# A decode step of sliding-window attention mixed with a gated MLP: TensorE's loop over all eight key sets, wide last products, and two rows of wo loaded by DMAs of 121 and 7 partitions

## The chip, the cores and the metric

One core of a Trainium2 chip. The metric is the device time of one execution in microseconds, the median of several runs of the program. The engines are TensorE (PE, whose weight loads the profile lists as PEld), VectorE (DVE), ScalarE (ACT), GpSimd (POOL) and SyncE (SP). Here SP does nothing but issue the large loads, in order, and 16 DMA engines carry them out.

## The reference

```python
# B = 4, one query token, D = 512; 32 query heads, 8 key heads of 128, the last 4096 of 16384 keys; F = 1792
q = (x @ wq) -> [B, 32, 1, 128];  k, v = repeat of the last 4096 rows of each cache, 4 query heads to a key head
p = softmax(q @ k.T * 128 ** -0.5);   a = (p @ v) -> [B, 1, 4096] @ wo
gate = x @ W_gate;  gate = gate * (gate > 0);   b = (gate * (x @ W_up)) @ W_down
g = sigmoid((x * gate_w).sum(-1, keepdims=True))
return g * a + (1 - g) * b
```

All inputs and the output [4, 1, 512] are bf16.

## The kernel before

The work on the caches is cut into eight **sets** (`NSET`): set `s` is one batch element and half of its eight key heads, 4 MB of keys and 4 MB of values. Each cache has two buffers of 4 MB in SBUF (`Ksb`, `Vsb`), used in turn.

**The load queue.** SP issues in this order: wq (into `Wbig`, ahead of everything else), K0, K1, V0, K2, V1, ..., K7, V6, W_gate and W_up (into the place of an even K), V7, W_down (into the place of an even V), then wo into `Wbig` in pieces of 16, 10 and 4 rows a partition (`WO_CUTS`, L245) and two half-width pieces of the last 2 rows (L248). A load of K for set s waits for the last scores of set s-2 (`SC`, L222), a load of V for the last value products of set s-2 (`PV`, L226). The first loads into a buffer wait for nothing. SP is in order, so a load that waits holds back all behind it.

**A set on the engines.** `kt` (L363): 64 fp32 transposes of 128x128 turn the keys (two bf16 seen as one fp32) on PE, four to a PSUM bank; ACT (L368) or DVE (L370) copies each bank back over the keys. `scores` (L384): four banks of 8 products 32x512; DVE adds a mask and takes the maximum (L392). `maximum` (L398 to L403) finds one maximum for each row, with one product on PE. `exponent` (ACT, L411) and `turn` (a DVE transpose, L418) prepare the weights of the set before in two halves, `values` (L429) multiplies them with V in four groups of 16 products, ACT copies the result (L435), and `combine` (L443, L447, L450, L451) sums and scales it into `oq`. One set's transposes and scores are interleaved with the exponents and values of the set before, and the combine of the one before that; the order is written out by hand.

**PE's program.** `Program` collects each engine's operations with the semaphore values that they wait for. The operations of sets 0 and 1 stand in PE's program one by one; sets 2 to 7 are a hardware loop of three turns, two sets to a turn (`LOOP_FIRST`, `LOOP_TURNS`, `turn_edge`, `emit`, L134). At the end of a turn PE drains and takes a turn's counts off the semaphores. The other engines' programs have no loop.

**Ahead of the sets.** POOL builds identities, masks and zeroed tiles. x and the gate's row are widened, transposed by PE, and copied by DVE into `gwB` and `xT`; PE then computes the gate (ACT's sigmoid) and q: 32 products with wq (L314), a copy by ACT (L324), transposes (L332), copies by DVE and ACT (L338).

**The end.** After set 7's loop part: its exponents, `gateup` (L459) with W_gate and W_up, ReLU and product on ACT and DVE, the value products of set 7, its combine. Then `product` (L530) adds 14 rows of W_down and 32 rows of wo to one PSUM bank `AB`: for each row four products, one to each quarter of the 512 columns, on four column groups of PE:

```python
        for i in range(NFT):
            for cb in range(4):
                product(hT[:, 4 * i:4 * i + 4], Wd[:, i, :], cb, i == 0, False, None,
                        [("WD",), ("H",), ("SCC", NSET - 1, NBANK - 1)])
        for k in range(len(WO_CUTS) - 1):
            for i in range(WO_CUTS[k], WO_CUTS[k + 1]):
                for cb in range(4):
                    product(oq3[:, :, i], Wo3[:, i, :], cb, False, False, None, [("WO", k), ("OQ", NSET - 1)])
```

DVE and ACT copy the four quarters to `outr`, and SP stores it (L574).

Of the kernel before, what the change touches and what calls it, by code (L numbers as in the profile page):

```python
# [31 lines left out]
WO_CUTS = (0, 16, 26, 30)  # L32
ACT_TAKES = (0, 1, 4, 6, 8, 9, 11, 12, 13, 14, 15)
LOOP_FIRST = 2
LOOP_TURNS = 3


class Program:

# [8 lines left out]
    def __init__(self):  # L48
        self.ops = {e: [] for e in self.ENGINES}
        self.events = {}  # L50
        self.counts = {}
        self.history = {}
        self.dmas = []
        self.turns = []
        self.shared = {}

    def op(self, engine, fn, name=None, waits=(), sem=None):
        if name is not None:
            assert name not in self.events, name
            sem = sem or engine  # L60
            self.counts[sem] = self.counts.get(sem, 0) + 1
            self.events[name] = (sem, self.counts[sem], engine, len(self.ops[engine]))
            self.history.setdefault(sem, []).append(len(self.ops[engine]))
        self.ops[engine].append((fn, name, tuple(waits), False))

# [12 lines left out]
    def need(self, engine, waits):  # L78
        need = {}
        for w in waits:  # L80
            if w is None:
                continue
            s, n, by, at = self.events[w]
            for own, mine in (("dve", "vd"), ("act", "va")):
                want = mine if engine == "pe" else own
                if by == own and s in (own, mine) and s != want:
                    s = want
                    n = 1 + sum(1 for k in self.history[s] if k < at)
                    assert n <= self.counts[s], w
            need[s] = max(need.get(s, 0), n)  # L90
# [6 lines left out]
    def emit_list(self, eng, sems, engine, ops, shift, seen):  # L97
        for fn, name, waits, is_dma in ops:
# [5 lines left out]
            if fn is None:  # L104
                continue
# [17 lines left out]
    def emit(self, engine, eng, sems):  # L123
# [6 lines left out]
        first = self.signature(ops[t[0]:t[1]], {})  # L130
        for k in range(1, len(t) - 1):
            shift = {s: k * n for s, n in self.lowered.items() if s not in self.shared}
            assert self.signature(ops[t[k]:t[k + 1]], shift) == first, k
        with eng.Fori(0, len(t) - 1):  # L134
            self.emit_list(eng, sems, engine, ops[t[0]:t[1]], {}, {})
# [3 lines left out]
        shift = {s: (len(t) - 1) * n for s, n in self.lowered.items() if s not in self.shared}  # L139
        self.emit_list(eng, sems, engine, ops[t[-1]:], shift, {})  # L140


def bass_gated_mix__sliding_block_cached__glu_gated_reglu__decode_kernel(
# [13 lines left out]
    with ExitStack() as ctx:  # L157
# [7 lines left out]
        pT = sb("pT", [128, 2, 2048], BF16)  # L165
# [11 lines left out]
        xT = sb("xT", [128, 4, 32], BF16)  # L177
        xw = sb("xw", [5, 512], FP32)
        gwB = sb("gwB", [128, 512], BF16)
        gsb = sb("gsb", [128, 8], FP32)  # L180
        qW = sb("qW", [128, NSET, 2, 32], BF16)
        qS = sb("qS", [128, 2, 2, 32], BF16)
        mx = sb("mx", [128, 2, NBANK], FP32)
        mcol = sb("mcol", [128, 2], FP32)
# [3 lines left out]
        rowsum = sb("rowsum", [128, 2, NPIECE], FP32)  # L188
        osb = sb("osb", [128, 2, 256], FP32)
# [5 lines left out]
        hT = sb("hT", [128, NFT * 4], BF16)  # L195
        outr = sb("outr", [4, 512], BF16)
        banks = [ctx.enter_context(nc.psum_tensor("bank%d" % i, [128, 512], FP32)) for i in range(8)]
# [9 lines left out]
        Wq3 = Wbig[:, :].rearrange("p (t w) -> p t w", t=4)  # L207
# [4 lines left out]
        def loop_sem(kind, s):  # L212
            if kind == "K" and s >= LOOP_FIRST or kind == "V" and LOOP_FIRST - 1 <= s < NSET - 1:
# [11 lines left out]
        def load_v(s):  # L225
            P.dma("sp", lambda e: e.dma_start(Vsb[:, s % 2, :], heads(A_v_cache, s)), ("V", s),  # L226
                  [("PV", s - 2, 3)] if s >= 2 else [], sem=loop_sem("V", s))
# [14 lines left out]
        wo_src = A_wo.rearrange("(p i) w -> p (i w)", p=128)  # L242
        for k in range(len(WO_CUTS) - 1):
            lo, hi = 512 * WO_CUTS[k], 512 * WO_CUTS[k + 1]
            P.dma("sp", lambda e, lo=lo, hi=hi: e.dma_start(Wbig[:, lo:hi], wo_src[:, lo:hi]), ("WO", k), [("Q",)])  # L245
        wo_src3 = A_wo.rearrange("(p i) w -> p i w", p=128)
        for u in range(2):
            P.dma("sp", lambda e, u=u: e.dma_start(Wo3[:, WO_CUTS[-1]:32, 256 * u:256 * u + 256],  # L248
                                                   wo_src3[:, WO_CUTS[-1]:32, 256 * u:256 * u + 256]), ("WOL", u), [("Q",)])
# [8 lines left out]
        P.op("pool", lambda e: e.memset(xw[:, :], 0.0), ("XW0",))  # L258
        P.op("pool", lambda e: e.memset(xT[:, :, :].rearrange("p t r -> p (t r)"), 0.0))
        P.op("pool", lambda e: e.memset(qW[:, :, :, :].rearrange("p s h w -> p (s h w)"), 0.0), ("QZ",))  # L260
# [34 lines left out]
        for t in range(4):  # L295
            P.op("pe", lambda e, t=t: e.transpose(FB[:, t * 8:t * 8 + 5], xv[0:5, t, :], identw[0:5, 0:5]),  # L296
                 ("XT",) if t == 3 else None, [("XW",), ("IDENTW",)])
        P.op("dve", lambda e: e.tensor_copy(gwB[:, :].rearrange("p (t m) -> p t m", t=4),
                                            fx[:, :, 4:5].to_broadcast([128, 4, 128])),
             None, [("XT",)])  # L300
        P.op("dve", lambda e: e.tensor_copy(xT[:, :, 0:4], fx[:, :, 0:4]), ("XTC",), [("XT",), ("QZ",)], sem="vd")
        for t in range(4):
            P.op("pe", lambda e, t=t: e.matmul(FB[:, 32:36], gwB[:, t * 128:(t + 1) * 128], xT[:, t, 0:4],
                                               start=(t == 0), stop=(t == 3)),
                 ("Z",) if t == 3 else None, [("XTC",)])
# [31 lines left out]
        for cc in range(2):  # L337
            P.op(("dve", "act")[cc], lambda e, cc=cc: (e.copy if cc else e.tensor_copy)(  # L338
                qW[64 * cc:64 * cc + 64, :, :, 16 * cc:16 * cc + 16].rearrange("p s o j -> p (s o) j"),
                FB[64 * cc:64 * cc + 64, 64:320].rearrange("p (k j) -> p k j", j=16)),  # L340
                ("QC", cc), [("QT",), ("QZ",)])
# [5 lines left out]
        fills = []  # L347

        def copy_done(f):
            return ("KTC",) + fills[f]  # L350

        def kt(s, i):
            f = len(fills)
            fills.append((s, i))
            bk = TR[f % NTR]
            for cc in range(4):
                c = 4 * i + cc
                w = []
                if cc == 0:
                    w = [("K", s), ("IDENTW",)] + ([copy_done(f - NTR)] if f >= NTR else [])  # L360
                    if i == NTR - 1 and s >= 1:
                        w.append(("NEGMAX", s - 1))
# [9 lines left out]
        def scores(s, bank):  # L372
# [4 lines left out]
            for o in range(2):  # L377
                for a in range(4):
                    w = []
                    if a == 0 and o == 0:  # L380
                        w = [("KTC", s, 4 * bank + u) for u in range(4)] + [("QS", s)]
                        if prev >= 0:
                            w.append(("SCC", prev // NBANK, prev % NBANK))
# [12 lines left out]
        def maximum(s):  # L396
            par = s % 2
            P.op("dve", lambda e: e.tensor_reduce(mcol[:, par:par + 1], mx[:, par, :], AXIS.X, ALU.max),  # L398
                 ("MCOL", s), [("SCC", s, NBANK - 1), ("MT", s - 2) if s >= 2 else None], sem="vd")
            P.op("pe", lambda e: e.matmul(TR[NTR - 1][:, 0:128], mcol[:, par:par + 1].to_broadcast([128, 128]), identw[:, :],  # L400
                                          start=True, stop=True),
                 ("MT", s), [("MCOL", s), ("KTC", s, NFILL - 1)])
            P.op("dve", lambda e: e.tensor_tensor_reduce(  # L403
                mrow[:, :], TR[NTR - 1][:, 0:128], qmask[:, :], -SCALE, -LOWEST, ALU.add, ALU.min, negmax[:, par:par + 1]),
# [4 lines left out]
        def exponent(s, k):  # L409
            par = s % 2  # L410
            P.op("act", lambda e: e.activation(  # L411
                sc[:, par, k * PW:(k + 1) * PW], sc[:, par, k * PW:(k + 1) * PW], ACTF.Exp,
                bias=negmax[:, par:par + 1], scale=SCALE, accum_out=rowsum[:, par, k:k + 1]),
                ("EXP", s, k), [("NEGMAX", s), ("SUMS", s - 2) if s >= 2 else None])

        def turn(s, k):
            par = s % 2
            P.op("dve", lambda e: e.transpose(pT[:, par, k * PW:(k + 1) * PW], sc[:, par, k * PW:(k + 1) * PW]),  # L418
                 ("PTT", s, k), [("EXP", s, k), ("PV", s - 2, 3) if s >= 2 else None], sem="vd")

        def values(s, k):
            par = s % 2
            for c in range(16):
                g = c % 4
                w = []
                if c == 0:
                    w = [("PTT", s, k * NPIECE // 4), ("V", s), ("OSB", s - 1) if s >= 1 else None]
# [6 lines left out]
            if k == 3:  # L434
                P.op("act", lambda e: e.copy(osb[:, par, :], OB[:, 0:256]), ("OSB", s),  # L435
                     [("PV", s, 3), ("SUMS", s - 2) if s >= 2 else None], sem="va")

        def combine(s):
            par, b, half = s % 2, s // 2, s % 2
            r = slice(64 * half, 64 * half + 64)  # L440
            for k in range(8):
# [3 lines left out]
                     [("OSB", s), ("WSUM",), ("OQ", s - 1) if s >= 1 else None])  # L445
            for k in range(NPIECE):
                P.op("pe", lambda e, k=k: e.matmul(FB[r, 416:417], Wsum[:, :], rowsum[:, par, k:k + 1],  # L447
                                                   start=(k == 0), stop=(k == NPIECE - 1)),
                     ("SUMS", s) if k == NPIECE - 1 else None, [])
            P.op("dve", lambda e: e.reciprocal(recip[r, par:par + 1], FB[r, 416:417]), ("RECIP", s), [("SUMS", s)])  # L450
# [4 lines left out]
        def gateup():  # L455
            for which, W, key in ((0, Wg, "WG"), (1, Wu, "WU")):
                for t in range(4):
                    for g in range(4):
# [4 lines left out]
                            [(key,)] + [copy_done(f) for f in range(NSET * NFILL - NTR, NSET * NFILL)])  # L463
# [7 lines left out]
                hT[:, :].rearrange("p (i b) -> p i b", b=4),  # L471
# [5 lines left out]
        for i in range(NFILL):  # L477
            kt(0, i)
            if i % 4 == 3 and i > 3:
                scores(0, i // 4 - 1)  # L480
        scores(0, 3)
        for s in range(1, NSET):
            if s >= LOOP_FIRST and (s - LOOP_FIRST) % 2 == 0:
# [12 lines left out]
            if s >= 2:  # L496
                combine(s - 2)
# [35 lines left out]
        for i in range(NFT):  # L533
            for cb in range(4):
                product(hT[:, 4 * i:4 * i + 4], Wd[:, i, :], cb, i == 0, False, None,
                        [("WD",), ("H",), ("SCC", NSET - 1, NBANK - 1)])
        for k in range(len(WO_CUTS) - 1):
            for i in range(WO_CUTS[k], WO_CUTS[k + 1]):
                for cb in range(4):
                    product(oq3[:, :, i], Wo3[:, i, :], cb, False, False, None, [("WO", k), ("OQ", NSET - 1)])  # L540
# [12 lines left out]
        per = {}  # L553
        for s in ("vd", "va"):
            eng = {"vd": "dve", "va": "act"}[s]
            a = P.events[("KTC", LOOP_FIRST, next(i for i in range(NFILL) if (i in ACT_TAKES) == (s == "va")))][1]
            b = P.events[("KTC", LOOP_FIRST + 2, next(i for i in range(NFILL) if (i in ACT_TAKES) == (s == "va")))][1]
            per[s] = b - a
        per["pq"] = 2
# [3 lines left out]
        P.lowered = per  # L563

# [3 lines left out]
        nc.sync.dma_start(Wbig[:, :], A_wq.rearrange("(p t) w -> p (t w)", p=128)).then_inc(sems["wq"], 16)  # L568
# [51 lines left out]
```

## Time and profile before

| | |
|---|---|
| median of 3 runs | 196.13 us (196.07 to 196.14) |
| the profiled execution | 196.17 us, of which the trace spans 194.9 |
| TensorE products, weight loads | 139.4 us (72%), 103.6 us (53%) |
| VectorE, ScalarE, GpSimd | 77.2 us (40%), 76.1 us (39%), 9.5 us (5%) |
| loaded from HBM | 81.01 MB, 416 GB/s over the span |
| mean granted clock of TensorE | 0.889 |

The shares are of the span. In the profile's rows of 40 slices each digit is the busy share of a slice in tenths; a slice is 4.9 us. A line of the timeline gives the start and the duration in us, the engine, the line of the kernel, the operation, output and inputs, the number of instructions, and in brackets how long the engine was idle before it and what released it. `SPq` is SP's queue issuing a DMA. In the queue list, q1 carries the loads that SP issues, q8 and q14 are queues that fetch instructions.

### The profile page before, as it was taken

What the parts mean: (1) busy time and instruction counts of PE and PEld (TensorE: products, weight loads), DVE (VectorE), ACT (ScalarE), POOL (GpSimd) and SP (SyncE); (2) the same over time, 40 slices, a digit from 0 to 9 for tenths busy, and PEclk for the clock granted to TensorE, in tenths of its full rate; (3) what the DMA queues carried; (4) which work ended last, traced back from release to release, by engine and by line L of the source; (5) the groups of instructions that cost most, each with busy time, mean ns of one, the idle gap of its engine ahead of it and who ended that gap; (6) DMA issues with size and microseconds to landing.
All of it is one profiled execution on the core that took longest, in us unless ns stands there. A gap on an engine that the chain in (4) does not pass through costs nothing.

```text
span 194.9 us, 3931 instructions
## 1 busy us (share of the span) xinstructions
PE 139.4 (72%) x1728; PEld 103.6 (53%) x1728; DVE 77.2 (40%) x169; ACT 76.1 (39%) x140; POOL 9.5 (5%) x41
## 2 busy tenths in 40 slices
PE   0135399688789818996898189995995899643834
PEld 0112397366468517763685177854773777422633
DVE  0100045477268302762583026623952456280101
ACT  2005136494285404462854043445641545240001
POOL 8700000000000000000000000000000000000000
PEclk9999999999999995899999855799999579995855
DMA  6999999999999999999999999999999999998993
GB/s 216 444 437 430 430 444 434 430 430 430 440 430 417 437 427 430 437 437 427 430 430 444 430 437 430 430 430 430 430 430 430 430 386 427 479 430 381 429 397 102
DMA packets 3884, 81.16 MB, mean 416 GB/s; under 512 B 409, under 2 KB 930, under 8 KB 1058
## 3 DMA queue, kind: packets, MB, share of 16 engines
q1 hardware_dynamic: 3864, 81.01, 97.3%
q8 instruction: 8, 0.13, 0.3%
q14 instruction: 2, 0.02, 0.0%
q10 hardware_dynamic: 10, 0.01, 0.0%
HBM read 81.01 MB, written 0.00 MB: 416 GB/s over the span
## 4 chain that ended last, share of the span: by engine, by line
DMA 55%; PE 36%; ACT 4%; DVE 3%; issue 1%; SPq 1%; DVEq 0%
DMA Ksb<-in_A_k_cache_dram 43%; PE bank L363 23%; DMA Wbig<-in_A_wo_dram 11%; PE bank L384 6%; ACT Ksb L368 3%; PE bank L429 2%; PE bank L443 2%; DVE Ksb L370 1%; PE bank L530 1%; ACT L411 1%; ACT sc L411 1%; DVE pT L418 1%; PE bank L447 0%; DVE sc L392 0%; PE bank L400 0%
## 5 line engine op out<-in xcount | busy, mean ns | idle before, releaser
L363 PE MATMUL bank<-identw,Ksb 128*128 128x128 f32 x512 | 77.0, 307 | 20.8 <-DMA Ksb<-in_A_k_cache_dram 14.9
L363 PEld LDWEIGHTS bank<-identw,Ksb 128*128 128x128 f32 x512 | 65.3, 158 | 31.6 <-DMA Ksb<-in_A_k_cache_dram 15.8
L368 ACT COPY Ksb<-bank 128x512 f32<-128x512 f32 x88 | 48.7, 589 | 73.0 <-PE bank L363 73.0
L370 DVE COPY Ksb<-bank 128x512 f32<-128x512 f32 x40 | 27.3, 684 | 40.6 <-PE bank L363 40.6
L392 DVE CUSTOM_DVE_ANT_0 sc<-bank,mask 128x512 bf16<-128x512 f32 x32 | 21.8, 682 | 28.8 <-PE bank L384 28.8
L429 PE MATMUL bank<-Vsb,pT 128*32 128x256 bf16 x512 | 20.9, 291 | 6.1 <-DMA Vsb<-in_A_v_cache_dram 6.1
L384 PE MATMUL bank<-Ksb,qS 128*32 128x512 bf16 x256 | 21.0, 405 | 1.8 <-ACT Ksb L368 0.9
L418 DVE STREAM_TRANSPOSE pT<-sc 128x1024 bf16<-128x1024 bf16 x16 | 19.7, 1236 | 2.1 <-ACT sc L411 2.0
L429 PEld LDWEIGHTS bank<-Vsb,pT 128*32 128x32 bf16 x512 | 13.3, 101 | 12.6 <-issue 8.8
L411 ACT ACTIVATE sc<-sc,negmax 128x1024 bf16<-128x1024 bf16 x16 | 18.4, 1151 | 1.9 <-DVE negmax L403 1.8
L443 PEld LDWEIGHTS bank<-osb,Wsel 128*64 128x64 f32 x128 | 9.4, 157 | 4.8 <-issue 3.7
L443 PE MATMUL bank<-osb,Wsel 128*64 128x32 f32 x128 | 10.3, 239 | 0.5 <-ACT osb L435 0.5
L435 ACT COPY osb<-bank 128x256 f32<-128x256 f32 x8 | 3.0, 373 | 17.6 <-PE bank L429 17.6
L400 PE MATMUL bank<-identw,mcol 128*128 128x128 f32 x16 | 3.8, 320 | 7.8 <-DVE mcol L398 4.7
L384 PEld LDWEIGHTS bank<-Ksb,qS 128*32 128x32 bf16 x256 | 4.1, 95 | 9.0 <-ACT Ksb L368 5.7
L400 PEld LDWEIGHTS bank<-identw,mcol 128*128 128x128 f32 x16 | 2.4, 187 | 10.2 <-DVE mcol L398 8.4
L343 POOL COPY qS<-qW 128x64 bf16<-128x64 bf16 x8 | 1.8, 238 | 120.5 <-PE bank L384 110.8
L530 PE MATMUL bank<-Wbig,oq 128*4 128x128 bf16 x128 | 4.2, 307 | 3.8 <-DMA Wbig<-in_A_wo_dram 3.8
L296 PE MATMUL bank<-identw,xw 5*128 5x5 f32 x4 | 0.6, 263 | 8.6 <-DVE xw L290 8.6
L450 DVE RECIPROCAL recip<-bank 64x1 f32<-64x1 f32 x8 | 1.3, 159 | 11.4 <-PE bank L447 11.4
L530 PEld LDWEIGHTS bank<-Wbig,oq 128*4 128x4 bf16 x128 | 3.1, 118 | 4.8 <-DMA Wbig<-in_A_wo_dram 4.7
L314 PE MATMUL bank<-Wbig,xT 128*32 128x512 bf16 x32 | 3.6, 631 | 2.7 <-DMA Wbig<-in_A_wq_dram 2.7
(55 smaller groups left out, 45.4 us busy)
## 6 DMA issues: line engine op xcount, KB each, us to landing
Ksb<-in_A_k_cache_dram SPq DMA_DIRECT2D x8, 4096.0 KB, 21.8
Vsb<-in_A_v_cache_dram SPq DMA_DIRECT2D x8, 4096.0 KB, 30.9
Wbig<-in_A_wq_dram SPq DMA_DIRECT2D x1, 4096.0 KB, 12.2
Wbig<-in_A_wo_dram SPq DMA_DIRECT2D x1, 2048.0 KB, 19.5
Ksb<-in_B_W_gate_dram SPq DMA_DIRECT2D x1, 1792.0 KB, 17.1
Ksb<-in_B_W_up_dram SPq DMA_DIRECT2D x1, 1792.0 KB, 21.0
Vsb<-in_B_W_down_dram SPq DMA_DIRECT2D x1, 1792.0 KB, 15.0
Wbig<-in_A_wo_dram SPq DMA_DIRECT2D x1, 1280.0 KB, 22.1
```

The costliest lines, as they stand in the source:

```text
L314: P.op("pe", lambda e, half=half, t=t, g=g, col=col: e.matmul(SCB[half][32 * g:32 * g + 32, 0:512], xT[:, t, :], Wq3[:, t, col:col + 512], ...
L363: P.op("pe", lambda e, bk=bk, cc=cc, c=c, s=s: e.transpose(bk[:, cc * 128:(cc + 1) * 128], Kw[:, s % 2, c * 128:(c + 1) * 128], identw[:, :]),
L368: P.op("act", lambda e: e.copy(dst, bk[:, :]), ("KTC", s, i), [("KT", s, i)], sem="va")
L370: P.op("dve", lambda e: e.tensor_copy(dst, bk[:, :]), ("KTC", s, i), [("KT", s, i)], sem="vd")
L384: P.op("pe", lambda e, a=a, o=o: e.matmul(bk[32 * a:32 * a + 32, 0:512], qS[:, s % 2, o, :], k4[:, 16 * bank:16 * bank + 16, 32 * a:32 * a ...
L392: P.op("dve", lambda e: e.tensor_tensor_reduce(sc[:, s % 2, bank * 512:(bank + 1) * 512], bk[:, :], mask[:, :], 1.0, LOWEST, ALU.add, ALU.max,
L400: P.op("pe", lambda e: e.matmul(TR[NTR - 1][:, 0:128], mcol[:, par:par + 1].to_broadcast([128, 128]), identw[:, :], start=True, stop=True) ...
L411: P.op("act", lambda e: e.activation(sc[:, par, k * PW:(k + 1) * PW], sc[:, par, k * PW:(k + 1) * PW], ACTF.Exp, bias=negmax[:, par:par + ...
L418: P.op("dve", lambda e: e.transpose(pT[:, par, k * PW:(k + 1) * PW], sc[:, par, k * PW:(k + 1) * PW]), ("PTT", s, k), [("EXP", s, k), ("PV ...
L429: P.op("pe", lambda e, c=c, g=g, blk=blk: e.matmul(OB[32 * g:32 * g + 32, 0:256], pT[:, par, 32 * blk:32 * blk + 32], Vsb[:, par, 256 * bl ...
L443: P.op("pe", lambda e, k=k, lo=lo: e.matmul(FB[r, 384:416], Wsel[:, lo:lo + 64], osb[:, par, 32 * k:32 * k + 32], start=(k == 0), stop=(k ...
L530: P.op("pe", lambda e: e.matmul(AB[32 * cb:32 * cb + 4, 0:128], stat, mov[:, 128 * cb:128 * cb + 128], start=start, stop=stop, tile_positi ...
```

## The change

- PE's loop now covers all sets: four turns of two sets. For the first turn, sets -2 and -1 are given as blanks: PE runs their products on a tile `zs` that POOL has zeroed in one memset, and DVE and ACT execute a 1-element instruction where an operation of a blank set would only raise a semaphore (`signal`, `blank`). PE adds a turn's counts to some semaphores before the loop (`ahead`).
- wq is loaded into the second V buffer instead of `Wbig`, so V1's load waits for the value products of blank set -1, and wo's loads wait for nothing.
- The product of `maximum` goes to a score bank, and the first scores of a set wait for it instead of the fourth bank of transposes.
- W_down and the first 16 rows of wo are multiplied in products of 512 columns, row n on column group n % 4 of a bank of its own; ACT copies that bank to `bulk`, and four fp32 products with `S32` add its four groups to `AB`, queued after the rows 26 to 29 of wo.
- The first two of wo's 16 rows a partition come by DMAs of their own, one for partitions 0 to 120 and one for 121 to 127, ahead of a DMA with the other 14.
- The copies to `gwB`, `xT` and both of q's move to ACT.

```diff
+BULK_PIECES = 1
+ODD_ROWS = 2
-LOOP_FIRST = 2
-LOOP_TURNS = 3
...
+        for s, n in self.ahead.items():
+            eng.sem_inc(sems[s], n)
         with eng.Fori(0, len(t) - 1):
-            self.emit_list(eng, sems, engine, ops[t[0]:t[1]], {}, {})
+            self.emit_list(eng, sems, engine, ops[t[0]:t[1]], shift(0), {})
             eng.drain()
...
-        Wq3 = Wbig[:, :].rearrange("p (t w) -> p t w", t=4)
+        Wq3 = Vsb[:, 1, :].rearrange("p (t w) -> p t w", t=4)
...
             P.dma("sp", lambda e: e.dma_start(Vsb[:, s % 2, :], heads(A_v_cache, s)), ("V", s),
-                  [("PV", s - 2, 3)] if s >= 2 else [], sem=loop_sem("V", s))
+                  [("PV", s - 2, 3)] if s >= 1 else [], sem=loop_sem("V", s))
...
+        for k, r in enumerate((slice(0, 121), slice(121, 128))):
+            P.dma("sp", lambda e, r=r: e.dma_start(Wbig[r, 0:512 * ODD_ROWS], wo_src[r, 0:512 * ODD_ROWS]), ("WOD", k))
         for k in range(len(WO_CUTS) - 1):
-            lo, hi = 512 * WO_CUTS[k], 512 * WO_CUTS[k + 1]
+            lo, hi = 512 * max(WO_CUTS[k], ODD_ROWS), 512 * WO_CUTS[k + 1]
...
-        P.op("pool", lambda e: e.memset(xw[:, :], 0.0), ("XW0",))
-        P.op("pool", lambda e: e.memset(xT[:, :, :].rearrange("p t r -> p (t r)"), 0.0))
-        P.op("pool", lambda e: e.memset(qW[:, :, :, :].rearrange("p s h w -> p (s h w)"), 0.0), ("QZ",))
+        P.op("pool", lambda e: e.memset(zs[:, 1024:], 0.0), ("XW0",))
...
         def maximum(s):
             par = s % 2
-            P.op("dve", lambda e: e.tensor_reduce(mcol[:, par:par + 1], mx[:, par, :], AXIS.X, ALU.max),
-                 ("MCOL", s), [("SCC", s, NBANK - 1), ("MT", s - 2) if s >= 2 else None], sem="vd")
+            if s < 0:
+                P.signal("dve", ("MCOL", s), "vd")
+            else:
+                P.op("dve", lambda e: e.tensor_reduce(mcol[:, par:par + 1], mx[:, par, :], AXIS.X, ALU.max),
+                     ("MCOL", s), [("SCC", s, NBANK - 1), ("MT", s - 2)], sem="vd")
...
-        for i in range(NFILL):
-            kt(0, i)
-            if i % 4 == 3 and i > 3:
-                scores(0, i // 4 - 1)
-        scores(0, 3)
-        for s in range(1, NSET):
-            if s >= LOOP_FIRST and (s - LOOP_FIRST) % 2 == 0:
+        P.events[("V", -1)] = ("V1", 16, None, 0)
+        for s in range(NSET):
+            if s % 2 == 0:
                 P.turn_edge()
...
-        for i in range(NFT):
-            for cb in range(4):
-                product(hT[:, 4 * i:4 * i + 4], Wd[:, i, :], cb, i == 0, False, None,
-                        [("WD",), ("H",), ("SCC", NSET - 1, NBANK - 1)])
-        for k in range(len(WO_CUTS) - 1):
+        DB = SCB[1]
+        rows = [(hT[:, i, :] if i < 4 else hT[:, i, 0:4], Wd[:, i, :], [("WD",), ("H",), ("SCC", NSET - 1, NBANK - 1)])
+                for i in range(NFT)]
+        for k in range(BULK_PIECES):
+            rows += [(oq3[:, :, i], Wo3[:, i, :], [("WO", k), ("WOD", 0), ("WOD", 1), ("OQ", NSET - 1)])
+                     for i in range(WO_CUTS[k], WO_CUTS[k + 1])]
+        for n, (stat, mov, waits) in enumerate(rows):
+            g = n % 4
+            P.op("pe", lambda e, g=g, n=n, stat=stat, mov=mov: e.matmul(
+                DB[32 * g:32 * g + (32 if n < 4 else 4), 0:512], stat, mov, start=(n < 4), stop=(n >= len(rows) - 4),
+                tile_position=(0, 32 * g)), ("BULK",) if n == len(rows) - 1 else None, waits)
+        P.op("act", lambda e: e.copy(bulk[:, :], DB[:, :]), ("BULKC",), [("BULK",)], sem="va")
+        for k in range(BULK_PIECES, len(WO_CUTS) - 1):
             for i in range(WO_CUTS[k], WO_CUTS[k + 1]):
                 for cb in range(4):
-                    product(oq3[:, :, i], Wo3[:, i, :], cb, False, False, None, [("WO", k), ("OQ", NSET - 1)])
+                    product(oq3[:, :, i], Wo3[:, i, :], cb, i == WO_CUTS[BULK_PIECES], False, None,
+                            [("WO", k), ("OQ", NSET - 1), ("NEGMAX", NSET - 1)])
+        for cb in range(4):
+            product(S32[:, 0:4], bulk, cb, False, False, None, [("BULKC",), ("WSUM",)])
...
-        nc.sync.dma_start(Wbig[:, :], A_wq.rearrange("(p t) w -> p (t w)", p=128)).then_inc(sems["wq"], 16)
+        nc.sync.dma_start(Vsb[:, 1, :], A_wq.rearrange("(p t) w -> p (t w)", p=128)).then_inc(sems["wq"], 16)
```

## The prediction

> **What bounds the kernel now.** I read the page's slices and queues first, then SyncE's own timeline, then the end of the span.
>
> ```profile
> PE   0135399688789818996898189995995899643834
> PEclk9999999999999995899999855799999579995855
> DMA  6999999999999999999999999999999999998993
> ...
> q1 hardware_dynamic: 3864, 81.01, 97.3%
> q8 instruction: 8, 0.13, 0.3%
> q14 instruction: 2, 0.02, 0.0%
> ```
>
> The DMA row is full from the second slice to the last but three: the load queue keeps the 16 DMA engines at work 97.3% of the span, and TensorE has slices at 1 and 3 tenths. So the kernel is one stream of 81.0 MB; a 32 KB packet takes 1.22 us on one engine, 16 engines together 430 GB/s. Only three things can move the end: a hole in the stream, how unevenly the 16 engines finish, and what follows the last landing.
>
> No hole opens while SyncE issues each load before the ones queued ahead are through. Two tight issues, and the wait at the loop's back-edge beside the same place inside a turn:
>
> ```profile
> 22.72 6.57 PE L363 MATMUL bank<-identw,Ksb 128*128 128x128 f32 x32 [4.50 <-DMA Ksb<-in_A_k_cache_dram]
> ...
> 35.68 0.53 SPq L222 DMA_DIRECT2D Ksb<-in_A_k_cache_dram  x1
> ...
> 51.03 0.54 SPq L222 DMA_DIRECT2D Ksb<-in_A_k_cache_dram  x1
> ...
> 68.26 0.49 PE L400 MATMUL bank<-identw,mcol 128*128 128x128 f32 x2 [0.56 <-DVE mcol L398]
> ...
> 91.81 0.46 PE L400 MATMUL bank<-identw,mcol 128*128 128x128 f32 x2 [1.57 <-issue]
> ```
>
> The trace also holds every DMA packet, and an engine starts one within 4 ns of the end of the one before, so each engine's stream can be followed. Each of the 16 closes its share of a transfer with a 4-byte write. The first transfer closes between 12.14 and 12.65 us, a spread of 0.51. Then PE's code arrives on q8: 16 KB packets at 31.7, 51.0, 59.9, 69.5, 89.9, 182.3, 188.7 and 192.4 us, 1.00 to 1.17 us each, each holding up one engine's data (q14's two, at 60.7 and 61.0, 0.4 us each). At 80 us the spread is 2.03: ten engines lie within 0.39 of the first, six at 1.26 to 2.03. The first piece of wo closes from 185.21 to 187.27: eight engines within 0.41, eight at 1.31 to 2.06, mean 0.97. The last data packet ends at 190.35 at the earliest on an engine that lost nothing, at 192.37 on the latest. So the stream ends about 1.0 us after its mean, and the latest engine decides.
>
> ```profile
> 190.91 2.30 PE L530 MATMUL bank<-Wbig,oq 128*4 128x128 bf16 x64 [1.25 <-DMA Wbig<-in_A_wo_dram]
> 192.13 0.52 PEld L530 LDWEIGHTS bank<-Wbig,oq 128*4 128x4 bf16 x20 [0.27 <-DMA Wbig<-in_A_wo_dram]
> 192.82 0.10 PEld L530 LDWEIGHTS bank<-Wbig,oq 128*4 128x4 bf16 x4 [0.17 <-DMA Wbig<-in_A_wo_dram]
> 192.98 0.54 ACT L550 CAST outr<-bank 4x128 bf16<-4x128 f32 x2 [10.29 <-PE bank L530]
> 193.61 0.35 SPq L574 DMA_DIRECT2D out_dram<-outr  x1
> ```
>
> At the end TensorE waits for wo three times (190.91, 192.13, 192.82); 0.16 us after the last of them the output is cast and written, and 1.9 us later the span ends. TensorE is idle 2.57 us at 187.77 and 1.25 us at 190.91: narrower or wider products before that gain nothing by themselves.
>
> The profiled execution took 196.17 us (span 194.9), 0.04 above the median of 196.13. This kernel's measurement can tell about 0.2%, 0.39 us.
>
> **The change, part by part.**
>
> *PE's code.* The built programs hold 130,816 bytes of PE instructions before and 87,168 after: 7.98 and 5.32 packets of 16 KB. Three of eight disappear, so five engines instead of eight lose 1.06 us to them. On the mean that is 3 x 1.06 / 16 = 0.2 us; on the latest engine, nothing unless it is one that is spared. So alone: 0 to 0.2, and I take 0.
>
> *The two rows of wo.* 16 rows a partition came in one DMA (8 packets of 16,384 B per engine, 0.613 us each, 4.90). Now 14 rows come in packets of 14,336 B (0.539 us, 4.31) and two in 2 KB packets. The trace has no 2 KB packet; between 4,096 B at 0.159 and 1,024 B at 0.044, 0.08 us is near the larger one's rate. Every DMA of the trace gives equal whole rows to the engines it uses: 128 rows 8 each on 16, 4 rows one each on 4. The only equal split of 121 on at most 16 is 11 x 11, of 7 it is 7 x 1. So eleven engines get 11 x 0.08 = 0.88 us, seven of them (if the two sets overlap) 0.96, and five get nothing: an even share would be 8 x (0.613 - 0.539) = 0.59, so the five are relieved by 0.59 and the others get 0.29 to 0.37 more. [...]
>
> The latest engine now: if the five relieved engines are the five that lose a code packet, they stand at most at 0.51 + 1.16 - 0.59 = 1.08, the others at 0.51 + 0.37 = 0.88. Against 2.02 that is 0.94 earlier. If one code packet falls on a loaded engine that starts at 0.2 to 0.5: 1.06 + 0.3 + (0.2 to 0.5), 1.56 to 1.86, only 0.15 to 0.45 earlier. Worst, an engine that stands at 2.02 already is also loaded: 0.37 later. No view says which engine a code packet takes. What the rows say is that by 185 us eight packets (six of q8, two of q14) have made eight engines late, each once: they go round in some order instead of falling by chance. An order that begins at one end of the 16 puts five packets on the five engines of that end. [...]
>
> *The wide products.* Wd falls from 56 products (1.20 us at 184.0) to 14 wide ones; by 8 wide L384 products in 0.62 that is 1.1 us, in front of a wait that ends at 187.77: 0. Sixteen wo rows become 16 wide products, 1.24 us, or 2.5 at half the granted clock (PEclk shows 5 there), against 64 in 1.88; with ScalarE's copy of the bank (128x512, 0.59) they are through by 190.9 at the latest. Needed at 192.6, so 1.7 us of cover. But four fp32 products that add the four row groups are queued on PE behind the last rows' wait. Price of 8 passes: 0.23 by L530's 29 ns each, 0.56 to 0.74 by the fp32 passes of L443 (16 in 1.12) and L447 (4 in 0.37), 0.95 by L363 (16 in 1.90). I take 0.5, near L443, whose operands are the most alike. Chain: 192.13 + 16 products 0.42 + 0.5 + the first four late products 0.1 + the last four and the drain 0.1 = 193.25, against 192.98: 0.27 later (0 to 0.72), as both landings come earlier together.
>
> *The loop.* Sets 0 and 1 now run the loop's body, set 0 with the combine and value products of sets before it, on zeros. Set 0 took 35.68 - 22.72 = 12.96 us to its last scores. It gains a combine (16 passes in 1.12 to 1.69, 4 in 0.37: 1.5 to 2.1) and three groups of value products: from scores(2) to K's issue set 1 takes 51.03 - 46.90 = 4.13, set 0 took 35.68 - 34.11 = 1.57, and two fills (0.98) only change places: 1.6. So 16.1 to 16.7 us, K2 issued at 38.8 to 39.4. First packets come 1.03 us after an issue and all engines are fed after 1.7 (0.81, 1.84, 2.52 for wq): 39.8 to 41.1, and the queue ahead ends at 41.2 to 42.9. Hidden, by 0.1 us at the least, and the latest engines have most. V1's load waits for set 0's empty value products, 0.6 us behind K2, with K2's 9.7 us ahead of it. Set 1 then ends near 54.3 (15.4 us a set), K3 is fed by 56.0 and needed at 60.6. A first back-edge is added: 1.57 us of idle against 0.56, so 1.0 us; set 2 ends at about 72, and K4 is needed at 80. Hidden. All later sets start at K's landing, as before.
>
> *The start.* GpSimd's one large memset costs 0.51 x 2600 / 512 = 2.6 us instead of 1.22, done by 4.5; xw waits for the gate's row until 8.07. Moving copies to ScalarE adds a table load (1.28) before the sigmoid and 0.4 us to q: scores need q at 29, K0's fills start at 22.72. 0. Two more issues on SyncE (0.43 each) delay the last wo issues to 171; their turn comes at 185. 0.
>
> Sum: 196.17 - 0.94 + 0.27 = 195.50; on the runs' median, 195.46.
>
> **Rivals.**
>
> A. *Code packets on both kinds of engine* (no change). If one of the five falls on a loaded engine: -0.3 + 0.27, so 196.1. For: q14's two packets belong to other engines' code and need not keep PE's order. Against: eight hits without a repeat.
>
> B. *The split makes the late engine later* (slower). One mechanism: the latest engine, which already stands at 2.02, is among the eleven loaded ones, as it would be if the round of code packets began at their end. 0.37 + 0.27: 196.8. It decides as soon as the latest engine's share of the two rows exceeds the even 0.59 us.
>
> C. *A hole in the stream at K2* (slower). If set 0 takes over 18.5 us, the late engines run dry too, and each further us is a us: at 20 us, 195.46 + 1.5 = 197.0. For: TensorE's first transposes run at 205 ns against 119, and more of the new work may fall in that phase; the first back-edge has a code packet beside it (89.9) and 1.57 us of idle. [...] Against: the entry to the loop lies in the 4.5 us in which PE waits for K0 anyway.
>
> D. *No balance, only the longer tail*: if the 121 rows were spread as evenly as 128, 0.27 remains, 196.4: no change that can be measured.
>
> **How the numbers follow.** Forecast 0.58, A 0.13, B 0.16, C 0.07, D 0.06. The forecast's own ends: code packets spared as well and the fp32 products free, 196.13 - 0.94 - 0.2 = 195.0, and 0.2 more for a still better balance (the mean is 1.0 below the latest); fp32 at 0.95, 195.9. The range runs from 194.8 to 196.9 and takes in A, B and D; C lies outside. Faster: the forecast without its upper end, 0.56; same: that end, A and D, 0.21; slower: B and C, 0.23.
>
> **What would show it.** q8 with five packets; the closing writes of wo's pieces spread by about 1.1 instead of 2.06, the last data by 191.5; PE's fp32 products taking 0.5 between the last rows and the last half rows; K2's issue near 39 with no hole after it. A spread of 1.6 or more makes it A, of 2.3 B; an issue of K2 after 41, C; over 2.8 us between the last data and the span's end (2.5 now), fp32 products dearer than I put them.

## The result, and the profile after

The changed kernel takes 197.96 us (median of 4 runs, 197.56 to 198.21) against 196.13: a ratio of 1.0088, 95% interval 1.0076 to 1.01. It is slower by 1.83 us by the medians, where 195.46 was forecast and 196.9 was the upper end of the range. The profiled execution is the longest of the four: 198.21 us with a span of 197.0, 2.1 more than before.

The page of the changed kernel, DMA rows and queues:

```profile
DMA  6999999999999999999999999999999999999991
GB/s 220 439 446 452 446 433 423 426 423 433 423 426 423 426 433 433 433 426 439 439 433 433 433 433 433 433 439 426 433 426 426 433 405 438 435 419 368 353 388 50
...
q1 hardware_dynamic: 4010, 81.01, 97.1%
q8 instruction: 5, 0.08, 0.2%
...
q14 instruction: 2, 0.02, 0.0%
```

The stream still has no hole: the DMA row is at 9 from the second slice to the last but one, and PE's code comes in five packets instead of eight. But the rate falls to 368 and 353 GB/s in two slices from 177 us on, while the engines count as busy. The same stretch by windows; the last two columns are the mean share of the DMA engines and GB/s. Before:

```profile
168.00:180.00 12.00, 4.68 (x82) 3.49 (x86) 5.00 (x12) 3.05 (x6) 0.00 (x0) 0.81 0.96 410
180.30:185.30 5.00, 4.40 (x116) 3.32 (x104) 0.49 (x2) 0.37 (x1) 0.00 (x0) 0.81 1.02 428
185.30:190.00 4.70, 1.88 (x64) 1.60 (x64) 0.00 (x0) 0.00 (x0) 0.00 (x0) 0.54 0.98 402
```

After:

```profile
168.00:180.00 12.00, 3.55 (x69) 2.41 (x71) 4.41 (x7) 2.40 (x5) 0.00 (x0) 0.75 0.97 416
180.30:185.30 5.00, 4.53 (x64) 3.54 (x60) 0.30 (x2) 0.37 (x1) 0.00 (x0) 0.50 1.02 302
185.30:190.00 4.70, 2.04 (x22) 0.48 (x18) 0.19 (x1) 0.00 (x0) 0.00 (x0) 0.50 0.98 415
```

Up to 180 us, and again from 185.3 to 190, the two kernels move about the same; in the five microseconds between, 302 instead of 428 GB/s at the same DMA share. That is 0.63 MB short, 1.5 us at 430 GB/s. These are the microseconds in which the two rows of wo pass through the engines. W_down's first share closes at 180.31 us in both kernels. In the packet records the first 2 KB packets, up to 180.8 us, take 0.084 us. The later ones take 0.10 to 0.18, and the mean of all 128 is 0.127. Every packet of 14,336 B (W_down's and wo's) that begins between 180.45 and 184.5 us is slowed as well, from 0.54 to as much as 0.97 us. (One of 1.03 stands right behind a code packet, and e2 below, which is not slowed, has one like it.) The mean of the 152 after 180 us is 0.653. An estimate of the lost engine time: 128 x 0.043 + 152 x 0.113 = 22.7 us, over 16 engines 1.4 us. The last data packet ends at 193.97 us instead of 192.37: 1.60 later.

The end of the changed kernel:

```profile
193.78 0.32 PEld L565 LDWEIGHTS bank<-Wbig,oq 128*4 128x4 bf16 x16 [0.30 <-DMA Wbig<-in_A_wo_dram]
194.06 0.25 PEld L565 LDWEIGHTS bank<-bulk,S 128*4 128x4 f32 x8
194.16 0.64 PE L565 MATMUL bank<-bulk,S 128*4 128x128 f32 x8
...
194.59 0.43 PE L565 MATMUL bank<-Wbig,oq 128*4 128x128 bf16 x8
195.05 0.54 ACT L596 CAST outr<-bank 4x128 bf16<-4x128 f32 x2 [3.12 <-PE bank L565]
...
195.68 0.30 SPq L620 DMA_DIRECT2D out_dram<-outr  x1
```

Behind its last wait, which ends at 193.78, PE works without a pause: 16 products, the fp32 products, the last 8. The cast starts 1.08 us after the last data; before it was 192.98 - 192.37 = 0.61. So the later data and the longer tail make 1.60 + 0.47 = 2.07 of the span's 2.1 us. Nothing ahead of the two rows holds up the stream:

```profile
38.12 0.53 SPq L254 DMA_DIRECT2D Ksb<-in_A_k_cache_dram  x1
...
53.45 0.54 SPq L254 DMA_DIRECT2D Ksb<-in_A_k_cache_dram  x1
...
55.29 0.49 PE L427 MATMUL bank<-identw,zs 128*128 128x128 f32 x2 [1.45 <-DVE zs L425]
```

K2 and K3 are issued at 38.1 and 53.5 us, before the queue ahead of them ends, and the new back-edge shows as 1.45 us of idle at 55.29.

### The profile page after: what moved, and what is told of

Read it like the earlier page. It is cut to its first block, busy times and chain, and to the rows that moved or that the text cites. A ratio compares the mean times of both kernels' runs of the same rounds, so it can differ in the third digit from the quotient of the medians.

```text
span 197.0 us, 3998 instructions
## 1 busy us (share of the span) xinstructions
PE 143.6 (73%) x1752; PEld 107.3 (54%) x1752; DVE 75.7 (38%) x172; ACT 79.3 (40%) x146; POOL 10.6 (5%) x39
## 4 chain that ended last, share of the span: by engine, by line
DMA 58%; PE 37%; ACT 2%; DVE 1%; SPq 1%; issue 1%; DVEq 0%
DMA Ksb<-in_A_k_cache_dram 45%; PE bank L386 23%; DMA Wbig<-in_A_wo_dram 13%; PE bank L408 6%; PE bank L464 3%; PE bank L480 3%; ACT Ksb L391 2%; PE bank L565 1%; DVE Ksb L393 1%; PE bank L484 1%; SPq L276 0%; DVE sc L416 0%; PE bank L427 0%; SPq L614 0%; SPq L279 0%
## 5 line engine op out<-in xcount | busy, mean ns | idle before, releaser
L464 PE MATMUL bank<-Vsb,zs 128*32 128x256 bf16 x576 | 23.3, 289 | 8.4 <-DMA Vsb<-in_A_v_cache_dram 8.4
L464 PEld LDWEIGHTS bank<-Vsb,zs 128*32 128x32 bf16 x576 | 14.8, 100 | 15.8 <-issue 11.5
L453 DVE STREAM_TRANSPOSE zs<-sc 128x1024 bf16<-128x1024 bf16 x16 | 19.7, 1237 | 3.0 <-ACT sc L443 2.8
L480 PEld LDWEIGHTS bank<-zs,Wsel 128*64 128x64 f32 x160 | 10.8, 146 | 4.7 <-issue 3.6
L480 PE MATMUL bank<-zs,Wsel 128*64 128x32 f32 x160 | 12.0, 231 | 0.5 <-ACT zs L472 0.5
L472 ACT COPY zs<-bank 128x256 f32<-128x256 f32 x8 | 3.0, 373 | 19.9 <-PE bank L464 19.9
L427 PE MATMUL bank<-identw,zs 128*128 128x128 f32 x18 | 4.4, 323 | 8.1 <-DVE zs L425 7.9
L427 PEld LDWEIGHTS bank<-identw,zs 128*128 128x128 f32 x18 | 2.7, 186 | 10.4 <-DVE zs L425 10.1
L346 PE MATMUL bank<-Vsb,zs 128*32 128x512 bf16 x32 | 3.6, 629 | 3.1 <-DMA Vsb<-in_A_wq_dram 3.1
L433 DVE CUSTOM_DVE_ANT_0 mrow<-bank,qmask 128x128 f32<-128x128 f32 x8 | 2.3, 292 | 8.0 <-PE bank L427 8.0
## 6 DMA issues: line engine op xcount, KB each, us to landing
Wbig<-in_A_wo_dram SPq DMA_DIRECT2D x1, 1792.0 KB, 22.7
```

What stands on the lines that cost most here:

```text
L346: P.op("pe", lambda e, half=half, t=t, g=g, col=col: e.matmul(SCB[half][32 * g:32 * g + 32, 0:512], xT[:, t, :], Wq3[:, t, col:col + 512], ...
L427: P.op("pe", lambda e: e.matmul(SCB[0][:, 0:128], mcol[:, par:par + 1].to_broadcast([128, 128]), identw[:, :], start=True, stop=True), ("M ...
L464: P.op("pe", lambda e, c=c, g=g, blk=blk: e.matmul(OB[32 * g:32 * g + 32, 0:256], pT[:, par, 32 * blk:32 * blk + 32], Vsb[:, par, 256 * bl ...
L480: P.op("pe", lambda e, k=k, lo=lo: e.matmul(FB[r, 384:416], Wsel[:, lo:lo + 64], osb[:, par, 32 * k:32 * k + 32], start=(k == 0), stop=(k ...
```

## The experiments

Each was timed in five rounds beside the kernel before, on the same chip as it; the changed kernel's own row is the result above. Theory 1 is that the split into 121 and 7 partitions slows the DMA engines. The rivals are the loop (2), small packets as such (3), and the reading of HBM at a pitch of 32 KB.

| run | median us | before beside it | ratio, 95% interval | 2 KB packet, mean us | 14,336 B after 180 us | last data us |
|---|---|---|---|---|---|---|
| changed kernel | 197.96 | 196.13 | 1.0088 (1.0076 to 1.01) | 0.127 | 0.653 | 194.0 |
| e1_one_dma | 196.54 | 196.25 | 1.0018 (1.0009 to 1.0026) | none | 0.540 | 192.3 |
| e2_two_rows_128 | 196.67 | 196.25 | 1.002 (1.0011 to 1.0029) | 0.084 | 0.545 | 192.3 |
| e3_split_112_16 | 197.61 | 196.25 | 1.0069 (1.0057 to 1.0081) | 0.105 | 0.624 | 193.4 |
| e4_before_121_7 | 197.61 | 196.25 | 1.0074 (1.0062 to 1.0086) | 0.127 | 0.646 | 193.8 |
| e7_source_dense | 197.67 | 196.21 | 1.0074 (1.0061 to 1.0088) | 0.127 | 0.658 | 193.7 |
| e11_split_64_64 | 198.09 | 196.26 | 1.0102 (1.0086 to 1.0117) | 0.125 | 0.647 | 193.6 |
| e5_sum_earlier | 196.40 | 196.21 | 1.0007 (0.9998 to 1.0016) | none | 0.539 | see below |
| e9_sum_first | 196.09 | 196.26 | 0.9993 (0.9984 to 1.0002) | none | 0.540 | 192.1 |
| e6_loop_alone | 196.16 | 196.21 | 0.9998 (0.9989 to 1.0007) | none | 0.540 | 192.2 |
| e8_last_rows_one_dma | 196.31 | 196.21 | 1.0005 (0.9996 to 1.0014) | 0.085 | 0.540 | 192.2 |
| e10_loop_and_last | 196.21 | 196.26 | 1.0 (0.9991 to 1.0009) | 0.084 | 0.539 | 192.1 |
| e12_both_moves | 196.17 | 196.28 | 0.9997 (0.9988 to 1.0006) | 0.085 | 0.540 | 192.0 |

The packets and the last data are those of each run's profiled execution; in e8, e10 and e12 the 2 KB packets are the joined last rows. Where the 16 rows come in one DMA, the 14,336 B packets after 180 us are the last 18 to 26 of W_down.

**The split taken out, put into the kernel before, and replaced.** First the 16 rows in one DMA again (the waits for the two DMAs go too; `...` stands for code left out):

```diff
-ODD_ROWS = 2
+ODD_ROWS = 0
-        for k, r in enumerate((slice(0, 121), slice(121, 128))):
-            P.dma("sp", lambda e, r=r: e.dma_start(Wbig[r, 0:512 * ODD_ROWS], ...), ("WOD", k))
```

> The changed kernel with the first 16 rows of wo in one DMA of 128 partitions again; loop and wide products stay. Theory 1, the split into 121 and 7 partitions slows the engines that carry it and their neighbours: wo's packets run at 159 to 613 ns as before, the last data lands near 192.3, and only the longer tail (about 0.47 us, the fp32 products) is left: 196.4 to 196.7 us. Theory 2, the loop or the empty sets delay the stream: it stays near 197.9.

196.54, and the data end where they ended before. The reverse edit puts the two DMAs into the kernel before and changes nothing else:

> The kernel before with nothing but the two rows in DMAs of 121 and 7 partitions. Theory 1: the same slow packets, the last data 1.4 to 1.7 us later than before, 197.4 to 197.9 us. Theory 2 or an interaction with the loop: 196.1 to 196.4.

197.61, with the same loss of rate between 180.3 and 185.3 us:

```profile
180.30:185.30 5.00, 3.66 (x93) 2.93 (x85) 0.49 (x2) 0.37 (x1) 0.00 (x0) 0.89 1.02 305
```

The split alone costs the kernel before about 1.4 us, and taking it away gives the changed kernel 1.4 us back; the loop and the wide products are not needed for it. Next the same 2 KB packets in one DMA of 128 partitions:

```diff
-        for k, r in enumerate((slice(0, 121), slice(121, 128))):
+        for k, r in enumerate((slice(0, 128),)):
```

> The changed kernel with the two rows in one DMA of 128 partitions (2 KB packets as in the changed kernel, eight on each of 16 engines). Theory 1 in the form that the place of the partitions matters: 2 KB packets take the 0.084 us of the first ones in the changed kernel throughout, W_down's and wo's 14,336 B packets stay at 0.54, and the time is that of one DMA plus at most 0.1: 196.4 to 196.8. Theory 3, small packets are slow beside large ones: packets of 0.12 to 0.16 again, 197.4 or more.

196.67 with 0.084 us throughout: 2 KB packets and one more DMA are not the cost. Its window:

```profile
180.30:185.30 5.00, 4.53 (x63) 3.58 (x59) 0.27 (x2) 0.37 (x1) 0.00 (x0) 0.50 1.00 414
```

414 GB/s where the changed kernel has 302. The source, the destination and the packets are those of the changed kernel; what differs is that one DMA carries the 128 rows instead of two. Two DMAs one behind the other are not slow by themselves: the two half-width pieces at the end of wo are such a pair of 128 partitions, and their 512 B packets take 0.027 to 0.029 us in the kernel before. Two splits that can be dealt to all engines evenly (e3 in the edit; e11 has 64 in place of 112):

```diff
-        for k, r in enumerate((slice(0, 121), slice(121, 128))):
+        for k, r in enumerate((slice(0, 112), slice(112, 128))):
```

> The changed kernel with the two rows split into DMAs of 112 and 16 partitions: both can be dealt out evenly on 16 engines (7 and 1 rows each), so no engine is relieved, but an engine's seven partitions are not the eight it writes in a DMA of 128. Theory 1a, what slows is that engines write to partitions that other engines write at the same time: packets of 0.12 us or more and 14,336 B packets over 0.6, 196.9 to 197.9. Theory 1b, what slows is that five engines run ahead into the next DMA while eleven are busy: no slowing here, 196.4 to 196.8.

> The changed kernel with the two rows in DMAs of 64 and 64 partitions: both can be dealt out evenly on 16 engines, four rows each, so the load of each engine is that of one DMA of 128 and only the partitions that an engine writes differ. Theory of the partitions: half the engines write where others write, 2 KB packets over 0.1 us on the mean, 14,336 B packets after 180 us over 0.58, 197.0 to 198. If only uneven loads or counts that are no power of two slow it: 84 ns, 196.4 to 196.8.

197.61 and 198.09, with 16 closing writes for each of the two DMAs in both runs, so every engine takes part in both. If whole rows are dealt equally, each engine then carries the even load and none is spared, and 64 is a power of two; and yet they are about as slow as 121 and 7. Theory 1b falls. The 2 KB packets of e3 are slowed less (0.105 us on the mean), and its window shows 344 GB/s. The window of the split into halves:

```profile
180.30:185.30 5.00, 4.16 (x70) 2.74 (x62) 0.49 (x2) 0.37 (x1) 0.00 (x0) 0.82 1.01 308
```

Last, the other end of the transfer. The two DMAs read a dense stretch of wo instead of rows 32 KB apart, so these two rows a partition then hold other rows of wo (only the call that changes is shown):

```diff
-e.dma_start(Wbig[r, 0:512 * ODD_ROWS], wo_src[r, 0:512 * ODD_ROWS])
+e.dma_start(Wbig[r, 0:512 * ODD_ROWS], A_wo.rearrange("(p i) w -> p (i w)", i=ODD_ROWS)[r, :])
```

> The changed kernel, but the two DMAs of 121 and 7 partitions read 128 neighbouring pieces of 2 KB from the start of wo instead of the first 2 KB of every 32 KB (so these two rows a partition hold other rows of wo). Same engines, same partitions written. If the slowing is on the side of writing to SBUF: as the changed kernel, 197.5 to 198.2, 2 KB packets at 0.127 on the mean. If it is on the side of reading HBM at that pitch: 196.4 to 196.8.

197.67, the packets as slow as in the changed kernel (0.127). The pitch of the read is not the cause. What is left is the written side: in these five microseconds 414 GB/s when the rows come in one DMA of 128 partitions, as in every other large load, 302 to 344 when they are split over two. That the split is the cause is shown (196.54 and 196.67 us without it, 197.61 to 198.09 with it); that it acts by the deal of the rows to the engines, and where the engines write, is argued by elimination, since no run changes the written side alone and no trace shows which engine writes which partition.

Over the runs, two DMAs of 121 and 7, 112 and 16 or 64 and 64 partitions take 0.105 to 0.127 us a 2 KB packet on the mean, one of 128 takes 0.084. Through what the split acts is in no trace.

**The tail.** The fp32 products moved ahead of rows 26 to 29 of wo (e5) or ahead of rows 16 to 25 (e9), both with one DMA for the 16 rows. The edit is that of e9; in e5 they stand inside the loop, ahead of its last pass:

```diff
+        for cb in range(4):
+            product(S32[:, 0:4], bulk, cb, True, False, None, [("BULKC",), ("WSUM",), ("NEGMAX", NSET - 1)])
         for k in range(BULK_PIECES, len(WO_CUTS) - 1):
             for i in range(WO_CUTS[k], WO_CUTS[k + 1]):
...
-        for cb in range(4):
-            product(S32[:, 0:4], bulk, cb, False, False, None, [("BULKC",), ("WSUM",)])
```

> The changed kernel with one DMA for the 16 rows (as in the first experiment) and the four fp32 products moved ahead of rows 26 to 29 of wo, where PE waits for the load anyway. If the fp32 products behind the last wait cost what is left over the kernel before: 0.4 us less than the first experiment, 196.0 to 196.2, no different from the kernel before. If the tail is set by something else (the last data, which stand where they stood): 196.5 as in the first experiment.

> Loop and wide products with one DMA for the 16 rows, and the four fp32 products ahead of rows 16 to 25 of wo, so that both later waits of PE lie behind them. If the 0.2 us that stayed after the move ahead of rows 26 to 29 are the same products still standing between two waits: 196.1 to 196.2, as the loop alone. If the wide products cost in another way: 196.4.

196.40, then 196.09. Ahead of rows 26 to 29 there is a gap of only 0.3 us for the products (0.27 in the kernel before), so part of them still pushes the chain; ahead of rows 16 to 25 they stand where PE is idle for 1.2 us. The end of e9:

```profile
190.05 0.61 PE L563 MATMUL bank<-bulk,S 128*4 128x128 f32 x8 [0.69 <-ACT bulk L577]
190.58 2.37 PE L563 MATMUL bank<-Wbig,oq 128*4 128x128 bf16 x64
...
192.69 0.56 ACT L594 CAST outr<-bank 4x128 bf16<-4x128 f32 x2 [2.69 <-PE bank L563]
```

The last data end at 192.1 and the cast starts 0.6 us later, as before the change (0.61). From e1 to e9, timed on different chips beside 196.25 and 196.26, the four products were worth 0.45 us. The profiled execution of e5 is the slowest of its twelve (197.42, the others 196.16 to 196.55); its last data end at 193.35, and why is not settled.

**The loop alone**, with narrow products for all rows of W_down and wo, as in the kernel before:

> The loop over all sets alone: narrow products for W_down and all rows of wo as in the kernel before, one DMA for the 16 rows. If loop, empty sets and the code packets that they save change nothing: 196.0 to 196.3, q8 with 6 or 7 packets. If the spared packets help the latest engine: 195.6 to 195.9. If the loop costs time by itself: over 196.4.

196.16 against 196.21, with six code packets: neither gain nor loss. **The last two rows in one DMA** of 2 KB a partition, in the kernel of e5, of e6 and of e9:

```diff
-        for u in range(2):
-            P.dma("sp", lambda e, u=u: e.dma_start(Wo3[:, WO_CUTS[-1]:32, 256 * u:256 * u + 256], ...), ("WOL", u))
+        P.dma("sp", lambda e: e.dma_start(Wbig[:, 512 * WO_CUTS[-1]:16384], wo_src[:, 512 * WO_CUTS[-1]:16384]), ("WOL", 0))
```

> As the experiment with the fp32 products moved, and the last two rows of wo come in one DMA of 2 KB a partition instead of two with 512 B pieces (32 packets of 0.027 us on an engine become 8 of 0.084: 0.86 against 0.67). If the last landing sets the end: 0.1 to 0.2 us less than without, 195.9 to 196.0; all 8 last products then follow the last landing instead of 4, about 0.1 us back. If packet sizes do not matter here: the same or 0.1 more.

> The loop alone with narrow products, and the last two rows of wo in one DMA of 2 KB a partition. Moving them together took 0.1 us off in the kernel with wide products: 196.0 to 196.1 here, under the kernel before by less than can be told. If it was chance there: 196.2.

> Loop and wide products, fp32 products ahead of rows 16 to 25, one DMA for the 16 rows, and the last two rows of wo in one DMA. With the fp32 products off the tail 196.1 was measured; the joined last DMA gave 0.1 in one kernel and nothing in another: 196.0 to 196.2. Under 195.87, 0.2% below the kernel before, only if both gains add up and the latest engine comes earlier.

196.31 (0.09 under e5), 196.21 and 196.17: whatever the shorter transfer gives is within the noise. No version is faster than the kernel before by more than the noise; e9 comes nearest, 0.07% under it with an interval that reaches 0.02% over.

## Why the prediction was wrong

The step that failed is "the two rows of wo". Its split was right: 18 closing writes for the two DMAs (422 in all against 404), as 11 and 7 make. Its price for a 2 KB packet, 0.08 us, was right for one DMA of 128 partitions (0.084 in e2). What it put at nothing is that the two DMAs of 121 and 7 partitions are slowed, and their neighbours in the queue with them: 0.127 for the 2 KB packets, and 0.653 instead of the 0.539 it used for the 14,336 B packets beside them. Nothing came earlier: taken in order of time, each of the 16 closings is later, and the 14-row piece closes first at 186.18 us, where the first 16 rows closed at 185.21 before, and last at 188.87, a spread of 2.69 instead of the 1.1 forecast. The term entered the sum with -0.94 and measures +1.60. Its base, that the five engines spared by the split are the five that lose a code packet, was the author's estimate: no run shows which engines a DMA or a code packet takes; what the runs showed in its place is the first closing 0.97 us later than before and the last 1.60.

Without the slowing, too, the -0.94 was more than its rows support. It took the relieved engines at 0.51 + 1.16 - 0.59, with 1.16 for a code packet. But in the trace before, the 32 KB packet that begins as a code packet ends (32.68, 52.12, 61.01, 70.61 and 90.88 us) takes 1.66 to 1.76 us instead of 1.22, so a code packet costs its engine about 1.5 us. That fits the eight late engines, which stood 1.31 to 2.06 behind the first: on the mean 1.71, against 0.23 for the other eight. An estimate from these rows puts the relieved ones at up to 2.06 - 0.59 = 1.47, a gain of about 0.6 at the most.

The price of 0.539 came from a queue in which every load is a DMA of 128 partitions; none of SP's loads in the trace before had another count, and the ends of the range did not allow for that.

The other steps, in their order:

- *PE's code*: five packets, as forecast. V7 closes last at 177.96 instead of 178.09: 0.13 in one execution each, inside the 0 to 0.2 given, and the loop alone shows no gain in time.
- *Wide products*: hidden, as forecast (the copy of the bank ends at 191.9, the next wait at 192.5 in the changed kernel). The fp32 products were priced at 0.5 and take 0.53 from their first weight load to the next product (194.06 to 194.59). The longer tail was put at 0.27 and measures 0.47 by the trace, 0.45 by the timings of e1 and e9. The part that was mis-sized is the last eight products and the drain behind them: 0.2 in the sum, 0.46 in the trace (194.59 to 195.05). So the sign "over 2.8 us between the last data and the span's end" came true with 3.0, but not through dearer fp32 products.
- *The loop*: K2 at 38.1 (38.8 to 39.4 forecast), K3 at 53.5 (54.3), the back-edge 0.9 us dearer than the 0.56 of a plain turn (1.0 forecast). No hole, so rival C did not come. *The start*: nothing, as forecast.
- *Rivals*: A and D left the stream's rate alone. B had the slower side, and its sign, a spread over 2.3, came true, but by luck: it charged one late engine 0.37 us for its larger share, while all engines lost 1.4 us on the mean.

Whether the five engines that lose a code packet are the five that the split spares stays open: every split that could tell was covered by the slowing.

## What to carry to other kernels

In this full load queue, two DMAs that split the 128 partitions, 0.25 MB in all, cost about 1.0 to 1.6 us against the same kernel with one DMA (e3, the changed kernel and e11 against e1): keep DMAs of 128 partitions and change bytes per partition instead (e2, 0.13 us over e1). The fp32 products behind the last wait counted with 0.45 of their 0.53 us, and ahead of a wait that ends later with nothing (e9, 196.09 against 196.26); look for the wait with the largest idle time in front of it. A price read from packets was good only beside the kind of neighbours that they had when it was read: 0.539 there, 0.653 beside the split.

## What the runs showed of the hardware that had not been expected

At a DMA share of 1.02 in both kernels the rate fell to 302 GB/s from 428, with nothing in the share of busy time to tell it: the DMA row and its 9s count a slowed packet as work. A share for every engine does not help: two DMAs of 64 partitions, each with 16 closing writes, ran at 308 GB/s in the same window, where one DMA of 128 with the same packets ran at 414. The slowing also lasts much longer than the 0.9 us that the two rows should take on one engine (an estimate: 11 packets at 0.08), and the engines come to them at different times (W_down's shares close from 180.32 to 182.38 us in the kernel before): the 2 KB packets run from 180.32 to 184.33 us, a 14,336 B packet begun at 182.95 still took 0.74 us, and only those begun after 185.1 take 0.54 again.
